# An FNet and gMLP block: another order of high parts, Gelus, copies and row sums in the z1 stage

## The chip, the cores and the metric

The kernel runs on one core of a Trainium2 chip. Its metric is the time of one execution on the device in microseconds (us); the median over several executions is given. The core has a matrix engine (PE in the profile, its weight loads PEld), a vector engine (DVE), a scalar engine for activations and copies (ACT), a general engine that here computes little and issues DMAs (POOL), and a sequencer that only issues DMAs (SP). Each engine works through its own queue in program order and waits on semaphores for what other engines must have done.

## The reference

Two sublayers act on 2048 tokens of 512 channels. What matters is the second one:

```python
h = _layernorm(x) * (1 + cb) + sb          # x after the Fourier sublayer
z  = _gelu(h @ w_in)                       # 2048 x 512 by 512 x 1792
z1 = z[..., :896]
z2 = _layernorm(z[..., 896:])
g  = w_sp @ z2 + b_sp[:, None]             # 2048 x 2048 by 2048 x 896
x  = x + gb * ((z1 * g) @ w_out)
```

The Fourier sublayer in front of it (two products with 512 x 512 matrices, two with 2048 x 2048 matrices) is the same in both kernels. All data are 32-bit floats.

## The kernel before, in words

**Split products.** Each float operand is split into a high part (a copy on ACT to a rounded type) and a low part (operand minus high part, a subtraction on DVE). `matmul3` (lines 93 to 97) then issues three PE instructions: high by high (L95), high by low (L96), low by high (L97). A high part and its low part must be there before the second or third of them can start.

**Stages.** The loop over `n` below `N2` is the Fourier sublayer. The loop from `N2` to `N3` computes z1 (lines 1156 to 1174), the next one z2, then come the product with `w_sp` and the output.

**The z1 stage.** The 896 columns of z1 are six column tiles of 128 and a seventh. The six are made as a 2 x 2 block product with seven block products in place of eight: the rows h (transposed, tiles `TT[k, g]`, k a block of 128 channels, g a group of 512 tokens) are cut into a, b, c, d by halves of channels and tokens, the weights into four blocks of 256 channels by 384 columns. The products run in the order `YPROD = (1, 2, 6, 7, 4, 5, 3)`, with four values of n each: step r below is n - N2 = r, and an even step multiplies one pair of h tiles (half gg = 0 or 1 of the token groups) with three column tiles, 18 PE instructions, in banks 0 to 2 of PSUM for gg = 0 and 3 to 5 for gg = 1. So steps 4 and 6 are product 2, steps 8 and 10 product 6, steps 12 and 14 product 7, steps 16 and 18 product 4, steps 20 and 22 product 5.

**The sums.** The weights' sums are `form_v`; their high and low parts `hi_v(p)` and `lo_v(p)`, two buffers in turn. The rows' sums are `make_x` (line 211; it also splits c for the seventh tile), `make_d`, S2 in `form_t` (line 245: d minus the difference a - c), `sum_x11` (a plus S2, needed by product 7) and a fourth sum, b minus S2, needed by product 4, which `prep_lo` makes at line 306 behind each low part of product 7. `prep_hi(m)` makes the high part of tile m, and with it a sum that it needs; `prep_lo(m)` the low part. `ahead(n)` calls `prep_hi` for steps n + 4 and n + 5.

**What comes out of PSUM.** After product 1 ACT copies the three banks away (L750) and they go on accumulating. After product 2 they hold z1 of the first token half: ACT applies Gelu and stores the result (L710, POOL issues the DMA), then copies product 1 back into the banks (L743), and product 6 is accumulated on top.

**The seventh column tile.** `mm_f7(g, k, ...)` accumulates it for token group g over four channel blocks, in bank `6 + g % 2`: groups 0 and 2 share bank 6, groups 1 and 3 bank 7. Groups 0 and 1 get their last blocks at the head of steps 4 and 6 and their Gelu is issued right there. `mm_x(gg)` does the first half of groups 2 and 3; it is called behind steps 6 and 10.

**The order** is written out by hand. `at(n, f, ...)` puts a call on a list (lines 1137 to 1155); a step runs its list, in the order in which it was filled, ahead of its matrix products, then `ahead`, then what empties PSUM, then the low parts of the next steps. A tile buffer or a PSUM bank that is given out again is waited for until its last readers are done.

Of the kernel before, what the change touches and what calls it, by code (L numbers as in the profile page):

```python
# [10 lines left out]
AF = mybir.ActivationFunctionType  # L11
ALU = mybir.AluOpType
# [7 lines left out]
def fnet_gmlp_kernel(  # L20
# [32 lines left out]
    nc = tc.nc  # L53
# [6 lines left out]
    ND = D // P  # L60
    NF = FH // P
# [17 lines left out]
    def bank(k, name):  # L79
        return psum.tile([P, 512], F32, tag=f"bank{k}", bufs=1, name=name)  # L80
# [12 lines left out]
    def matmul3(acc, ah, al, bh, bl, first, last, go_on=False):  # L93

        nc.tensor.matmul(acc, ah, bh, start=first, stop=False, skip_group_check=go_on)  # L95
        nc.tensor.matmul(acc, ah, bl, start=False, stop=False, skip_group_check=go_on)  # L96
        nc.tensor.matmul(acc, al, bh, start=False, stop=last, skip_group_check=go_on)  # L97
# [25 lines left out]
    def at(n, f, *a):  # L123
        fill.setdefault(n, []).append((f, a))

    def run(n):
        for f, a in fill.pop(n, []):
            f(*a)
# [10 lines left out]
    N2 = 4 * len(src)  # L139
    YPROD = (1, 2, 6, 7, 4, 5, 3)  # L140
    NY = {p: N2 + 4 * i for i, p in enumerate(YPROD)}
# [52 lines left out]
    def prep(n):  # L194

        if n not in prepared:
            prepared.add(n)
            prep_hi(n + 3)
            prep_lo(n + 2)

    def slot(i, name, dtype=F32):
        return slots[0].tile([P, Q], dtype, tag=f"slot{i}", bufs=1, name=name)

    slots, TT, S2, XH = [], {}, {}, {}
# [50 lines left out]
    def sum_x11(gg):  # L255
        for kk in range(2):
            nc.vector.tensor_tensor(TT[kk, gg], TT[kk, gg], S2[gg, kk], op=ALU.add)

    highs, lows, SE = set(), set(), []

    def load_first():
# [6 lines left out]
    def prep_hi(n):  # L268
        if n >= NE or n in highs:
            return  # L270
        highs.add(n)
        if N2 <= n < N4:
            T[n] = form_t(n)
        else:
            b, k = divmod(n, 4) if n < N2 else (NB0 + (n - N4) // 4, (n - N4) % 4)
            if b != NB0:
                T[n] = blocks.tile([P, Q], F32, tag="t", bufs=2, name=f"t{n}")
            if b == NB0:
                assert n in T
            elif n >= N4:  # L280
                squares(T[n], stage[b][:, k % 2], k // 2)
            else:
                squares(T[n], stage[b], k)
        AH[n] = SE[2][:, n - N4] if N4 <= n < N4 + 4 else blocks.tile([P, Q], F32R, tag="ah", bufs=4, name=f"ah{n}")
        nc.scalar.activation(AH[n], T[n], AF.Copy)  # L285
        if not N2 <= n < N4 and k == 3:
            stage.pop(b)
            if b != NB0:
                load(b + 2)


    def prep_lo(n):
        if n >= NE or n in lows:
            return
        lows.add(n)
        if N2 <= n < N4 and n % 4 == 3:
            AL[n] = slot(0, f"al{n}", F32R) if slots else zrow[0].tile([P, Q], F32R, tag="z1u", bufs=6, name=f"al{n}")
        elif N4 <= n < N4 + 4:
            AL[n] = slot(9 + n - N4, f"al{n}", F32R)
        else:  # L300
            AL[n] = blocks.tile([P, Q], F32R, tag="al", bufs=3, name=f"al{n}")
        t = T.pop(n)
        nc.vector.tensor_tensor(AL[n], t, AH[n].bitcast(F32), op=ALU.subtract)  # L303
        gg, kk = divmod(n % 4, 2)
        if NY[7] <= n < NY[7] + 4:
            nc.vector.tensor_tensor(TT[2 + kk, gg], TT[2 + kk, gg], S2[gg, kk], op=ALU.subtract)


    p2 = ctx.enter_context(ExitStack())
# [277 lines left out]
    def norm_y(t, i):  # L587
        LN[t, i] = rows.tile([P, D], F32, tag="row", bufs=6, name=f"h2_{t}_{i}")
        apply(LN[t, i], X.pop((t, i)), NRM.pop((t, i)))

    def post_h(t, i):
        h2 = LN.pop((t, i))
        nc.vector.tensor_tensor(h2, h2, mods[4], op=ALU.mult)
        (nc.vector if t == NQ - 1 else nc.gpsimd).tensor_tensor(h2, h2, mods[3], op=ALU.add)
        LN[t, i] = h2
# [12 lines left out]
    ZT = {}  # L608
# [73 lines left out]
    def ahead(n):  # L682
        for m in (n + 4, n + 5):
            prep_hi(m)

    ZB = (0, 1, 2, 6, 3, 4, 5, 7)
    Z1 = {}

    def mm_f7(g, k, th, tl):

        if k == 0:
            ZT["f7", g] = bank(6 + g % 2, f"f7p{g}")
        matmul3(ZT["f7", g], W7[0][:, 0, k], W7[0][:, 1, k], th, tl, k == 0, k == ND - 1)
        if k == ND - 1:
            end_z1(g, NF - 1, ZT.pop(("f7", g)), out_row(g, NF - 1))

    def out_row(g, f, tag="z1o"):
        if tag == "z1o":
            return zout[0].tile([P, Q], F32, tag=tag, bufs=7, name=f"z1o{g}_{f}")
        return zrow[0].tile([P, Q], F32, tag=tag, bufs=6, name=f"z1o{g}_{f}")  # L700

    def natural(z):
        return z.rearrange("p (a k i) -> p k a i", a=4, i=32)

    def turned(z):
        return z.rearrange("p (k a i) -> p k a i", k=4, i=32)

    def end_z1(g, f, ps, z):
        if ps is not None:
            nc.scalar.activation(natural(z), turned(ps), AF.Gelu_apprx_tanh)  # L710
        else:
            nc.scalar.activation(z, z, AF.Gelu_apprx_tanh)
        nc.gpsimd.dma_start(z1_d[g][f], z)

    def mm_x(gg):
        for kk, (h, l) in enumerate(XH.pop(gg)):
            mm_f7(2 + gg, kk, h, l)

    def mm_z1(n):
        p = YPROD[(n - N2) // 4]  # L720
        gg = n % 4 // 2
        fresh = p in (1, 5)
        a = [(AH.pop(m), AL.pop(m)) for m in (n, n + 1)]
        if p in (2, 3):
            for kk, t in enumerate(a):
                mm_f7(gg if p == 2 else 2 + gg, 2 + kk, *t)
        for f in range(3):
            if fresh:
                ZT[gg, f] = bank(3 * gg + f, f"z1p{p}_{gg}{f}")
            cols = slice(f * P, (f + 1) * P)  # L730
            for kk, (th, tl) in enumerate(a):
                matmul3(ZT[gg, f], WJ[1, p][:, 0, kk, cols], WJ[1, p][:, 1, kk, cols], th, tl,
                        fresh and kk == 0, kk == 1, not fresh)
        if n != N2 + 6:
            ahead(n)
        for f in range(3):
            empty_z1(p, gg, f)
        if p == 1:
            for kk, t in enumerate(a):
                mm_f7(gg, kk, *t)  # L740
        if p == 2:
            for f in range(3):
                nc.scalar.activation(turned(ZT[gg, f]), natural(Z1.pop((1, gg, f))), AF.Copy)  # L743

    def empty_z1(p, gg, f):

        ps = ZT[gg, f]
        if p in (1, 6, 7):
            Z1[p, gg, f] = zrow[0].tile([P, Q], F32, tag="z1u" if p == 6 else "z1m", bufs=6, name=f"z1_{p}_{gg}{f}")
            nc.scalar.activation(natural(Z1[p, gg, f]), turned(ps), AF.Copy)  # L750
        elif p in (2, 4):
            g, f = gg, f + (3 if p == 4 else 0)
            end_z1(g, f, ps, out_row(g, f, "z1u" if p == 2 else "z1o"))
        else:
            z = Z1.pop((7 if p == 5 else 6, gg, f))
            nc.vector.tensor_tensor(natural(z), turned(ps), natural(z), op=ALU.add)
            end_z1(2 + gg, f + (3 if p == 5 else 0), None, z)
# [287 lines left out]
    for j, turn, weigh, row, fold, hi in ((0, (25, 26, 27, 28), (29, 29, 30, 30), 26, (34, 34, 35, 36), (38, 35, 36, 37)),  # L1045
# [8 lines left out]
        n = weigh[3] + (3 if j == 0 else 1)  # L1054
# [13 lines left out]
    for t in range(NQ):  # L1068
        n = 8 * NQ * (t + 1)
# [43 lines left out]
    def change_s():  # L1113
        p2.close()
        slots.append(ctx.enter_context(pool("slots", "right")))
        spre.append(ctx.enter_context(pool("spre", "right")))
        bpool.append(ctx.enter_context(pool("bpool", "right")))
# [23 lines left out]
    at(N2 + 3, load_t, 3)  # L1141
    at(N2 + 4, make_x, 0)
    at(N2 + 6, make_d)
    at(N2 + 8, make_x, 1)
    at(N2 + 8, sum_x11, 0)
    at(N2 + 10, sum_x11, 1)
    at(N2 + 9, form_v, 5)
    at(N2 + 10, form_v, 3)
    for i, p in enumerate(YPROD[2:]):
        at(N2 + 4 + 4 * i, hi_v, p)  # L1150
        at(N2 + 5 + 4 * i, lo_v, p)
    at(N2 + 20, form_w, 7)
    at(NY[3], hi_w, 1)
    at(NY[3] + 1, lo_w, 1)
# [1 line left out]
    for n in range(N2, N3):  # L1156
        prep(n)
        if n % 2 == 0:
            prep_lo(n + 3)
        run(n)  # L1160
        if n % 2 == 0:
            mm_z1(n)
            ahead(n)
            if n == N2:
                norm_y(NQ - 1, 3)
            prep_lo(n + 4)
            prep_lo(n + 5)
            if n == N2:
                post_h(NQ - 1, 3)
                turn_h(NQ - 1, 3)  # L1170
                change_s()
                zout.append(w0.enter_context(pool("zout")))
            if n in (N2 + 6, N2 + 10):
                mm_x((n - N2) // 10)

    zstack = ctx.enter_context(ExitStack())
    w0.close()
# [14 lines left out]
    for i, p in enumerate(PROD):  # L1192
        for k in range(8):
            n = NB[p] + 2 * k
# [11 lines left out]
    for f in range(NF):  # L1206
        n = N4 + 24 + 8 * f
# [109 lines left out]
```

## Time and profile before

| | |
|---|---|
| time, median of 3 runs | 942.41 us (942.01 to 942.84) |
| the profiled execution's own time | 942.69 us |
| its span, first to last instruction | 940.9 us |
| PE busy | 932.1 us, 99% of the span |
| PEld busy | 772.7 us, 82% |
| DVE busy | 738.3 us, 78% |
| ACT busy | 413.6 us, 44% |
| POOL busy | 195.8 us, 21% |
| the z1 stage on PE | from 448.53 us to about 520 us |
| PE busy from 446 to 490 us | 41.55 of 44 us |
| PE busy from 490 to 528 us | 38.00 of 38 us |

A line of a timeline gives the start, the duration, the engine, the line of the kernel, the operation, the tiles (out<-in) and how many instructions were merged into it; brackets at its end give the idle time ahead of it and what ended it. Durations overlap: the distance from one start to the next is what an instruction costs its engine, unless it waits. A line of the waits gives who waited for whom, the total in us, how often, and the longest.

### The profile page before, as it was taken

How to read it: one execution, taken by the hardware profiler on the slowest of the kernel's cores; microseconds unless marked ns; L12 is line 12 of the kernel's file. 1: busy time of each engine (PE TensorE's matmuls, PEld its weight loads, DVE VectorE, ACT ScalarE, POOL GpSimd, SP SyncE). 2: the span in 40 equal slices, each digit the busy share in tenths (PEclk: the TensorE clock that was granted, in tenths of full speed). 3: DMA queues.
4: the chain of work that ended last, by engine and by line, in shares of the span. 5: the costliest groups of instructions: out<-in, count | busy, mean ns of one | idle time of the engine just before them, and what ended most of it. 6: DMA issues, size and time to landing. Idle time of an engine off the chain costs nothing.

```text
span 940.9 us, 12362 instructions
## 1 busy us (share of the span) xinstructions
PE 932.1 (99%) x4114; PEld 772.7 (82%) x4114; DVE 738.3 (78%) x1201; ACT 413.6 (44%) x726; POOL 195.8 (21%) x372
## 2 busy tenths in 40 slices
PE   9999999999999999999989999999999999999998
PEld 5888888888888888888868999888888888888886
DVE  6899957778677677875888878899799889886662
ACT  4684424232132222222577678675545544331221
POOL 2330000114554165323414211332000000000000
PEclk9999999999999999999999999999999999999999
DMA  9994762647539977994777523344564466743541
GB/s 213 226 235 103 143 146 67 168 134 180 144 87 321 275 212 216 275 332 151 240 264 278 180 95 74 90 100 104 133 142 106 114 145 139 182 110 140 185 173 56
DMA packets 236592, 157.07 MB, mean 167 GB/s; under 512 B 131472, under 2 KB 203408, under 8 KB 236400
## 3 DMA queue, kind: packets, MB, share of 16 engines
q1 hardware_dynamic: 223008, 118.65, 50.5%
q0 software_dynamic: 12128, 37.11, 11.0%
q8 instruction: 32, 0.52, 0.2%
q10 hardware_dynamic: 1392, 0.52, 0.2%
q14 instruction: 32, 0.26, 0.1%
HBM read 119.54 MB, written 36.70 MB: 166 GB/s over the span
## 4 chain that ended last, share of the span: by engine, by line
PE 92%; DVE 2%; DMA 2%; ACT 1%; POOL 1%; issue 1%; SPq 1%; DVEq 0%; ACTq 0%; POOLq 0%
PE gp L95 12%; PE gp L96 12%; PE gp L97 12%; PE gw L97 10%; PE gw L96 10%; PE gw L95 10%; PE op L96 3%; PE op L95 3%; PE op L97 3%; PE yp L97 3%; PE yp L96 3%; PE yp L95 3%; PE z2p L97 2%; PE z2p L95 2%; PE z2p L96 2%; PE z1p L97 1%
## 5 line engine op out<-in xcount | busy, mean ns | idle before, releaser
L285 ACT ACTIVATE ah<-t 128x512 fp32r<-128x512 f32 x244 | 154.1, 632 | 369.7 <-DVE t L190 240.6
L303 DVE TENSOR_TENSOR al<-t,ah 128x512 fp32r<-128x512 f32 x244 | 164.5, 676 | 65.3 <-PE gp L96 38.8
L95 PE MATMUL gp<-ah,hh 128*128 128x512 f32 x496 | 192.9, 389 | 0.0
L96 PE MATMUL gp<-al,hh 128*128 128x512 f32 x496 | 192.9, 389 | 0.0
L97 PE MATMUL gp<-ah,hl 128*128 128x512 f32 x496 | 192.9, 389 | 0.0
L190 DVE STREAM_TRANSPOSE t<-stage 128x512 f32<-128x512 f32 x236 | 165.9, 703 | 6.9 <-DMA stage<-in_A_dft_seq_re_dram 3.0
L96 PE MATMUL gw<-al,bh 128*128 128x512 f32 x400 | 155.6, 389 | 0.0
L97 PE MATMUL gw<-ah,bl 128*128 128x512 f32 x384 | 149.5, 389 | 0.0
L95 PE MATMUL gw<-ah,bh 128*128 128x512 f32 x384 | 149.4, 389 | 0.0
L97 PEld LDWEIGHTS gp<-ah,hl 128*128 128x128 f32 x496 | 93.1, 188 | 19.4
L95 PEld LDWEIGHTS gp<-ah,hh 128*128 128x128 f32 x496 | 93.1, 188 | 19.4
L96 PEld LDWEIGHTS gp<-al,hh 128*128 128x128 f32 x496 | 93.1, 188 | 19.2
L96 PEld LDWEIGHTS gw<-al,bh 128*128 128x128 f32 x400 | 75.1, 188 | 15.7
L97 PEld LDWEIGHTS gw<-ah,bl 128*128 128x128 f32 x384 | 72.1, 188 | 15.0 <-DVE bl L852 0.3
L95 PEld LDWEIGHTS gw<-ah,bh 128*128 128x128 f32 x384 | 72.1, 188 | 15.0
L824 POOL DMA_DIRECT2D s_d<-sj x64 | 35.1, 548 | 103.8 <-DVE sj L816 80.2
L95 PE MATMUL yp<-hth,gh 128*128 128x512 f32 x128 | 49.8, 389 | 0.0
L96 PE MATMUL yp<-htl,gh 128*128 128x512 f32 x128 | 49.8, 389 | 0.0
L97 PE MATMUL yp<-hth,gl 128*128 128x512 f32 x128 | 49.8, 389 | 0.0
L605 POOL DMA_DIRECT2D ht_d<-hturn x62 | 40.9, 665 | 23.6 <-DVE hturn L601 19.6
L95 PE MATMUL op<-woh,uh 128*128 128x512 f32 x112 | 43.6, 389 | 0.0
L96 PE MATMUL op<-wol,uh 128*128 128x512 f32 x112 | 43.6, 389 | 0.0
(220 smaller groups left out, 1466.4 us busy)
## 6 DMA issues: line engine op xcount, KB each, us to landing
stage<-in_A_dft_seq_im_dram SPq DMA_DIRECT2D x64, 256.0 KB, 5.2
sj<-in_B_w_sp_dram SPq DMA_DIRECT2D x32, 512.0 KB, 7.6
s_d<-sj POOLq DMA_DIRECT2D x64, 256.0 KB, 4.1
stage<-s_d SPq DMA_DIRECT2D x128, 128.0 KB, 2.7
stage<-in_A_dft_seq_re_dram SPq DMA_DIRECT2D x60, 256.0 KB, 5.3
stage<-in_B_w_sp_dram SPq DMA_DIRECT2D x88, 128.0 KB, 3.0
wm<-in_w_mod_dram SPq DMA_DIRECT2D x16, 256.0 KB, 5.8
xr<-in_A_x_dram POOLq DMA_DIRECT2D x16, 256.0 KB, 4.6
```

The lines of the kernel that those rows point to most:

```text
L95: nc.tensor.matmul(acc, ah, bh, start=first, stop=False, skip_group_check=go_on)
L96: nc.tensor.matmul(acc, ah, bl, start=False, stop=False, skip_group_check=go_on)
L97: nc.tensor.matmul(acc, al, bh, start=False, stop=last, skip_group_check=go_on)
L190: nc.vector.transpose(dst.rearrange("p (b i) -> p b i", i=32), block[:, :, 32 * k:32 * k + 32])
L285: nc.scalar.activation(AH[n], T[n], AF.Copy)
L303: nc.vector.tensor_tensor(AL[n], t, AH[n].bitcast(F32), op=ALU.subtract)
L605: eng.dma_start(v[a, i], ht[32 * a:32 * a + 32].rearrange("c (b r) -> c b r", r=32))
L824: nc.gpsimd.dma_start(s_d[m, r, g][b * P:(b + 1) * P, :], a)
```

## The change

Only the z1 stage changes, in five points.

- In `mm_z1` the high parts of the next pair (`ahead`) stand in front of the Gelus also at step 6, where they stood behind Gelus and copies.
- After product 2 each bank's copy stands right behind that bank's Gelu, in place of three Gelus and then three copies. The Gelu of the seventh tile for groups 0 and 1 is no longer issued where its products end, but behind the three Gelus and copies of its step (`end_f7`).
- The sum b minus S2 leaves `prep_lo` and becomes `sum_x12`, listed at steps 12 and 14.
- The weights' high and low part for product 6 move from steps 4 and 5 to step 3; the weight sums for products 5 and 3 from steps 9 and 10 to 13 and 17.
- The second `make_x` moves from step 8 to step 10, and the second `mm_x` from behind step 10 to behind step 12.

```diff
+    def sum_x12(gg):
+        for kk in range(2):
+            nc.vector.tensor_tensor(TT[2 + kk, gg], TT[2 + kk, gg], S2[gg, kk], op=ALU.subtract)
...
         nc.vector.tensor_tensor(AL[n], t, AH[n].bitcast(F32), op=ALU.subtract)
-        gg, kk = divmod(n % 4, 2)
-        if NY[7] <= n < NY[7] + 4:
-            nc.vector.tensor_tensor(TT[2 + kk, gg], TT[2 + kk, gg], S2[gg, kk], op=ALU.subtract)
...
         matmul3(ZT["f7", g], W7[0][:, 0, k], W7[0][:, 1, k], th, tl, k == 0, k == ND - 1)
-        if k == ND - 1:
-            end_z1(g, NF - 1, ZT.pop(("f7", g)), out_row(g, NF - 1))
+        if k == ND - 1 and g > 1:
+            end_f7(g)
+
+    def end_f7(g):
+        end_z1(g, NF - 1, ZT.pop(("f7", g)), out_row(g, NF - 1))
...
-        if n != N2 + 6:
-            ahead(n)
+        ahead(n)
         for f in range(3):
             empty_z1(p, gg, f)
+            if p == 2:
+                nc.scalar.activation(turned(ZT[gg, f]), natural(Z1.pop((1, gg, f))), AF.Copy)
         if p == 1:
             for kk, t in enumerate(a):
                 mm_f7(gg, kk, *t)
         if p == 2:
-            for f in range(3):
-                nc.scalar.activation(turned(ZT[gg, f]), natural(Z1.pop((1, gg, f))), AF.Copy)
+            end_f7(gg)
...
-    at(N2 + 8, make_x, 1)
     at(N2 + 8, sum_x11, 0)
     at(N2 + 10, sum_x11, 1)
-    at(N2 + 9, form_v, 5)
-    at(N2 + 10, form_v, 3)
+    at(N2 + 12, sum_x12, 0)
+    at(N2 + 14, sum_x12, 1)
+    at(N2 + 13, form_v, 5)
+    at(N2 + 17, form_v, 3)
     for i, p in enumerate(YPROD[2:]):
-        at(N2 + 4 + 4 * i, hi_v, p)
-        at(N2 + 5 + 4 * i, lo_v, p)
+        at(N2 + 4 + 4 * i - (not i), hi_v, p)
+        at(N2 + 5 + 4 * i - 2 * (not i), lo_v, p)
+    at(N2 + 10, make_x, 1)
...
-            if n in (N2 + 6, N2 + 10):
-                mm_x((n - N2) // 10)
+            if n in (N2 + 6, N2 + 12):
+                mm_x((n - N2) // 12)
```

## The prediction

> **What bounds the kernel now.** First the page: the share of PE, then the chain that ended last. Then the waits of PE's weight loads over the whole span, to see where PE is not busy.
>
> ```profile
> span 940.9 us, 12362 instructions
> PE 932.1 (99%) x4114; PEld 772.7 (82%) x4114; DVE 738.3 (78%) x1201; ACT 413.6 (44%) x726; POOL 195.8 (21%) x372
> ...
> PEld z1p L97 <- DVE vj L644: 1.8, 1, 1.8
> ...
> PEld z1p L95 <- ACT ah L285: 1.1, 1, 1.1
> PEld z1p L96 <- DVE al L303: 0.5, 1, 0.5
> PEld z1p L95 <- ACT z1p L743: 0.5, 1, 0.5
> ```
>
> PE is the bound: whatever PE loses anywhere adds to the end. Past its start it loses time in the z1 stage alone, at four places: a low weight part (`lo_v`), a high and a low row part behind S2, and a copy into PSUM. The change can win no more than these. What they cost is read from PE's timeline, start to start:
>
> ```profile
> 470.06 0.39 PE L97 MATMUL z1p<-ah,vj 128*128 128x512 f32 x1
> 470.29 0.39 PE L95 MATMUL f7p<-xh,w 128*128 128x512 f32 x1
> ...
> 471.42 0.39 PE L97 MATMUL f7p<-xh,w 128*128 128x512 f32 x1
> 471.89 0.50 PE L95 MATMUL z1p<-ah,vj 128*128 128x512 f32 x1
> 472.23 0.40 PE L96 MATMUL z1p<-al,vj 128*128 128x512 f32 x1
> ...
> 475.88 0.39 PE L97 MATMUL z1p<-ah,vj 128*128 128x512 f32 x1
> 476.98 0.50 PE L95 MATMUL z1p<-ah,vj 128*128 128x512 f32 x1 [0.72 <-ACT ah L285]
> 477.71 0.50 PE L96 MATMUL z1p<-al,vj 128*128 128x512 f32 x1 [0.23 <-DVE al L303]
> 478.05 0.39 PE L97 MATMUL z1p<-ah,vj 128*128 128x512 f32 x1
> ...
> 483.31 0.39 PE L96 MATMUL z1p<-al,vj 128*128 128x512 f32 x1
> 485.12 0.50 PE L97 MATMUL z1p<-ah,vj 128*128 128x512 f32 x1 [1.42 <-DVE vj L644]
> 485.45 0.39 PE L95 MATMUL z1p<-ah,vj 128*128 128x512 f32 x1
> ...
> 488.89 0.39 PE L95 MATMUL z1p<-ah,vj 128*128 128x512 f32 x1
> ```
>
> An undisturbed matmul takes 0.23 (470.06 to 470.29). The disturbed distances are 0.47, 0.34, 1.10, 0.73, 0.34, 1.81 and 0.33, together 5.12; less seven times 0.23 that is **3.51 us lost**. (The matmul behind each wait also takes 0.33 to 0.34: an extra 0.11 per stall.) That is the most the change can give back, 0.37%. At 488.89 step 14 begins; up to there both kernels give PE the same work, with the second `mm_x` at another place.
>
> **The change part by part.** The number of instructions on every engine stays the same; all is order. So I walk ACT's and DVE's queues in the new order, by these rows:
>
> ```profile
> 463.09 1.55 ACT L750 ACTIVATE z<-z1p 128x512 f32<-128x512 f32 x3
> 464.52 1.16 ACT L218 ACTIVATE xh<-tt 128x512 fp32r<-128x512 f32 x2
> 465.56 0.86 ACT L640 ACTIVATE vj<-w1e 128x768 fp32r<-128x768 f32 x1
> 466.30 0.61 ACT L710 ACTIVATE z1o<-f7p 128x512 f32<-128x512 f32 x1
> 468.66 1.24 ACT L285 ACTIVATE ah<-s 128x512 fp32r<-128x512 f32 x2 [1.75 <-DVE s L245]
> 469.80 1.56 ACT L710 ACTIVATE z1o<-z1p 128x512 f32<-128x512 f32 x3
> 471.23 1.65 ACT L743 ACTIVATE z1p<-z 128x512 f32<-128x512 f32 x3
> 472.79 0.60 ACT L710 ACTIVATE z1o<-f7p 128x512 f32<-128x512 f32 x1
> ```
>
> ```profile
> 465.19 0.69 DVE L221 TENSOR_TENSOR xl<-tt,xh 128x512 fp32r<-128x512 f32 x1 [1.18 <-ACT xh L218]
> ...
> 467.86 1.29 DVE L245 TENSOR_TENSOR s<-tt,tt 128x512 f32<-128x512 f32 x2
> ...
> 470.54 0.95 DVE L644 TENSOR_TENSOR vj<-w1e,vj 128x768 fp32r<-128x768 f32 x1
> 471.40 1.29 DVE L234 TENSOR_TENSOR xd<-xb,tt 128x512 f32<-128x512 f32 x2
> ```
>
> *Weights of product 6 at step 3.* `hi_v` now takes ACT at 464.52 in front of the two xh copies; it holds ACT for 0.74 (465.56 to 466.30) and ends 0.86 later, at 465.38. `lo_v` stands in front of xl on DVE, waits for that, starts at about 465.41 and holds DVE for 0.86 (470.54 to 471.40). So xl starts at 466.27 in place of 465.19: **1.08 later**, and with it the chain behind it, S2 (467.86 becomes 468.94), its high parts (468.66 becomes 469.74), and the first Gelu (469.80 becomes 470.88). The time won on DVE at 470.54 has no one waiting for it.
>
> *Gelu, copy, Gelu, copy.* A Gelu holds ACT for 0.48 (1.43 for three), a copy for 0.52 (1.56 for three), if they are independent. Now each copy overwrites the bank that the Gelu just ahead of it reads. What such a dependence costs on ACT is shown by the nearest pair, at the kernel's start, where the second line reads what the first wrote:
>
> ```profile
> 7.13 0.81 ACT L119 ACTIVATE xn<-x,first 128x511 f32<-128x511 f32 x1 [3.04 <-POOL xn L990]
> 7.97 0.63 ACT L459 ACTIVATE hh<-xn 128x512 fp32r<-128x512 f32 x1
> ```
>
> The second starts 0.03 behind the end of the first. A Gelu of 0.60 then holds ACT for 0.63; the lower bound is 0.48. I take 0.63: a pair 1.15, three pairs 3.45.
>
> *The seventh tile's Gelu goes behind them.* It was through at 466.9; now it starts at 470.88 + 3.45 = 474.33 and ends 0.61 later, at 474.94. Who waits for it is the point: the first `mm_x` (group 2) starts a new sum in bank 6, which this Gelu (group 0) still has to read. That `mm_x` ran at 470.29, and PE's queue holds steps 8 and 10 behind it. With 0.03 for the handoff it starts at 474.97. The distance on PE is 474.97 - 470.06 = 4.91, and the next 0.34; less two times 0.23, **4.79 us newly lost** (4.34 with the lower bound of 0.48).
>
> *What was late before.* Step 8's copies are now all done at about 474.4, before PE comes. Step 10's high parts stand ahead of its Gelus, at 474.33 + 0.48 = 474.81; its Gelus start 1.14 later (468.66 to 469.80), at 475.95, and its copies end by 479.5. PE gets to step 10 at 474.97 + 0.11 + 24 x 0.227 = 480.5. `lo_v` of product 7, freed of the weight sum and of the b sums in front of it, comes behind step 6's seventh Gelu (475.95 + 3.45 = 479.40): `hi_v` at 479.88, step 12's high parts 0.74 later, at 480.6, their low parts at 481.3, `lo_v` from 482.5 to 483.5; PE wants it at 480.5 + 18 x 0.227 + 0.45 = 485.0. So all the old 3.51 goes, under cover of the new wait.
>
> *The rest.* The b sums, four instructions of 0.69, and the second `make_x` go to steps at which only PE's own pace (18 matmuls, 4.1 us) frees buffers. The weight sum for product 3, 0.95 us long by the row below, now stands in front of product 5's `lo_v`:
>
> ```profile
> 483.24 0.95 DVE L631 TENSOR_TENSOR w<-w1e,w 128x768 f32<-128x768 f32 x1
> 484.11 0.95 DVE L644 TENSOR_TENSOR vj<-w,vj 128x768 fp32r<-128x768 f32 x1
> ...
> 498.53 0.95 DVE L644 TENSOR_TENSOR vj<-w,vj 128x768 fp32r<-128x768 f32 x1
> ```
>
> Before, this part was done at 499.48, and step 20 wanted it at 488.89 + 54 x 0.227 + 0.45 = 501.6: a margin of 2.1, of which 0.87 is spent. At zero, then, with 1.2 left over. The stores behind the Gelus on POOL's queue move by a few us, and nobody reads them before the output. SP's queue keeps its order.
>
> *The clock.* PE will stand idle from about 470.4 (end of the last matmul) to 474.97, some 4.5 us. The longest idle time after the start was the one ahead of 485.12, 1.42 by the row, and the matmuls behind it ran at full pace. What a long one does can be seen only at the program's start:
>
> ```profile
> L388 PEld LDWEIGHTS busyp<-busy,ones x10: 191/337/338, 1.5 to 8.1; 128*128 128x128 f32 x10
> ...
> 6.79 0.34 PEld L388 LDWEIGHTS busyp<-busy,ones 128*128 128x128 f32 x1 [0.52 <-issue]
> 7.64 0.23 PEld L388 LDWEIGHTS busyp<-busy,ones 128*128 128x128 f32 x1 [0.52 <-issue]
> ...
> L95 PEld LDWEIGHTS z1p<-ah,vj x84: 186/188/189, 448.3 to 519.3; 128*128 128x128 f32 x84
> ```
>
> A weight load took 337 ns, against 188 ns in the z1 stage, and the issue distance was 0.85 (6.79 to 7.64), then 0.46 (to 8.1): about half pace, from 1.5 to 7.6, although the granted clock reads 1.00 there. Half pace for 6.1 us costs 3.05 us. So for a restart after 4.5 us the bounds are 0 and 3.05. With an idle time three times the longest that did no harm I hold a slow restart the likelier, and a shorter one than after the load of the program: I take the middle, **1.5 us**.
>
> [...]
>
> **The sum.** - 3.51 + 4.79 + 1.5 = +2.8 us. The profiled execution took 942.69 us (span 940.9 and 1.8 around it), 0.3 above the median 942.41, so the steps carry over: 942.41 + 2.8 = **945.2 us**.
>
> **Rivals.** *B: the wait at bank 6 without a slow restart.* For it: no idle time in this trace after the start has been followed by slow matmuls. Against it: none was longer than 1.42. - 3.51 + 4.79 = +1.28, 943.7 us; 943.2 with the lower bound of 0.48.
>
> *C, not slower: the first `mm_x` finds its bank free.* Against it: the bank's number, 6 + g mod 2, is 6 for both groups. For it: the Gelu needs nothing but ACT's queue. Even then little is won: PE would run `mm_x` at 470.29, wait 0.6 for step 8's first copy (472.17), 0.9 for step 10's first copy (477.2), and 1.7 for `lo_v` of product 7 (483.5), since ACT and DVE are the slower chain here: 3.2 lost in place of 3.51, 942.1 us. It decides against a loss if the Gelu ends 1.3 earlier than walked, by 473.6; a gain above 0.2% would need `lo_v` earlier too.
>
> *D: product 5's `lo_v` becomes late.* DVE's queue from step 12 on now holds the b sums, both weight sums and the sums of `w_sp`. If a load makes one of those late by more than the 1.2 left, PE waits before step 20: each us beyond is a us, so 944.7 on top of B and 946.2 on top of my sum for one.
>
> **How the numbers follow.** My case 0.54, B 0.26, C 0.09, D 0.11. A measurement of this kernel tells about 0.2%, 1.9 us, from no change. My case and D are slower by more than that (0.65); B lies within it, as does nearly half of C (0.30); the rest of C is faster (0.05), if its chain is shorter than walked as well. The range goes from B's lower bound, 943.2 less 0.1, to my case with the whole 3.05, 946.7, and a little of D: 943.1 to 947.0; it leaves out C and part of D.
>
> **What would show it.** In the profile after: the first matmul of f7p with xh starts near 475.0, its wait put down to ACT and the tile z1o; the waits on vj, on ah and on al of product 6 are gone; weight loads behind 475 last 0.34 for some 3 us. S2 starts at 468.9. If the f7p matmul starts by 471, or a Gelu of f7p stands ahead of the copies on ACT, I am wrong in the main step; if weight loads behind it last 0.19, B holds; a wait of step 20 on vj is D.

## The result and the profile after

The changed kernel takes 945.81 us (median of 9 executions, 944.92 to 946.99), the kernel before 942.57 us (9 executions, 942.01 to 943.9): the ratio is 1.0032, with a 95% interval from 1.0023 to 1.0042. It is slower, by 3.2 us in the medians. Predicted were 945.2 us. The profiled execution took 945.12 us, 0.7 below the median.

The page of the changed kernel, its first lines, and the waits of PE's weight loads from 440 to 535 us, the z1 stage:

```profile
span 943.3 us, 12366 instructions
PE 932.5 (99%) x4114; PEld 774.0 (82%) x4114; DVE 738.2 (78%) x1201; ACT 414.4 (44%) x726; POOL 195.2 (21%) x372
```

```profile
PEld f7p L95 <- ACT z1o L714: 4.9, 1, 4.9
```

The four waits of before are gone. One has taken their place, and it is longer than they were together. Lines have moved by a few: the Gelus of L710 are L714 now, the copies of L743 are L742, the low parts of L303 are L307, the lines L285 are L289, L644 is L645. PE's timeline around that wait:

```profile
469.76 0.39 PE L97 MATMUL z1p<-ah,vj 128*128 128x512 f32 x1
474.60 0.50 PE L95 MATMUL f7p<-xh,w 128*128 128x512 f32 x1 [4.45 <-ACT z1o L714]
474.93 0.47 PE L96 MATMUL f7p<-xl,w 128*128 128x512 f32 x1
475.19 0.63 PE L97 MATMUL f7p<-xh,w 128*128 128x512 f32 x1
475.62 0.63 PE L95 MATMUL f7p<-xh,w 128*128 128x512 f32 x1
...
478.18 0.56 PE L95 MATMUL z1p<-ah,vj 128*128 128x512 f32 x1
478.58 0.40 PE L96 MATMUL z1p<-al,vj 128*128 128x512 f32 x1
478.81 0.40 PE L97 MATMUL z1p<-ah,vj 128*128 128x512 f32 x1
```

The first `mm_x` (f7p with xh) stands 4.84 us behind the last matmul of step 6, and the next one 0.33 behind it: 4.84 + 0.33 less two times 0.23 is 4.71 us lost. Then come eight distances of 0.40 to 0.43 (475.19 to 478.58 is 3.39 us in place of 1.84): another 1.55 us. The clock shows it as well, in the table by stretches (the stretch, its length, PE's busy time and matmuls, weight loads, DVE, ACT, POOL, the granted clock, the DMA share and rate):

```profile
470.00:474.60 4.60, 0.15 (x2) 0.01 (x1) 3.70 (x6) 4.50 (x10) 1.68 (x3) 1.00 0.93 251
...
475.20:478.60 3.40, 3.40 (x10) 2.66 (x9) 2.40 (x4) 3.31 (x7) 1.26 (x3) 0.51 1.05 414
478.60:482.00 3.40, 3.40 (x16) 2.79 (x15) 0.02 (x1) 2.29 (x5) 1.08 (x2) 1.00 1.04 411
```

For 3.4 us PE had half the clock (0.51 from 475.20 to 478.60). In the page's 40 slices, where the clock stays at 9 tenths or more throughout, this cannot be seen. What PE waited for is on ACT, here in the new order:

```profile
464.16 0.85 ACT L641 ACTIVATE vj<-w1e 128x768 fp32r<-128x768 f32 x1
464.89 1.16 ACT L218 ACTIVATE xh<-tt 128x512 fp32r<-128x512 f32 x2
469.38 1.23 ACT L289 ACTIVATE ah<-s 128x512 fp32r<-128x512 f32 x2 [3.33 <-DVE s L245]
470.52 0.58 ACT L714 ACTIVATE z1o<-z1p 128x512 f32<-128x512 f32 x1
471.13 0.60 ACT L742 ACTIVATE z1p<-z 128x512 f32<-128x512 f32 x1
471.67 0.58 ACT L714 ACTIVATE z1o<-z1p 128x512 f32<-128x512 f32 x1
...
473.96 0.58 ACT L714 ACTIVATE z1o<-f7p 128x512 f32<-128x512 f32 x1
474.44 1.14 ACT L289 ACTIVATE ah<-s 128x512 fp32r<-128x512 f32 x2
```

and, ahead of its high parts of S2, on DVE:

```profile
465.05 0.96 DVE L645 TENSOR_TENSOR vj<-w1e,vj 128x768 fp32r<-128x768 f32 x1 [1.35 <-ACT vj L641]
465.92 0.69 DVE L221 TENSOR_TENSOR xl<-tt,xh 128x512 fp32r<-128x512 f32 x1
...
468.58 1.29 DVE L245 TENSOR_TENSOR s<-tt,tt 128x512 f32<-128x512 f32 x2
```

The seventh tile's Gelu (z1o from f7p) runs from 473.96 to 474.54, and 0.06 later PE goes on. From 469.38 on ACT works with no gap over 0.03: that Gelu waits for nothing but its turn.

### The profile page after: what moved, and what is told of

It reads as the page before. It is cut to its first block, busy times and chain, and to the rows that moved or that the text cites. A ratio compares the mean times of both kernels' runs of the same rounds, so it can differ in the third digit from the quotient of the medians.

```text
span 943.3 us, 12366 instructions
## 1 busy us (share of the span) xinstructions
PE 932.5 (99%) x4114; PEld 774.0 (82%) x4114; DVE 738.2 (78%) x1201; ACT 414.4 (44%) x726; POOL 195.2 (21%) x372
## 4 chain that ended last, share of the span: by engine, by line
PE 93%; DVE 3%; ACT 1%; issue 1%; POOL 1%; DMA 1%; SPq 0%; ACTq 0%; DVEq 0%; POOLq 0%
PE gp L97 12%; PE gp L95 12%; PE gp L96 12%; PE gw L97 10%; PE gw L96 10%; PE gw L95 10%; PE op L97 3%; PE op L95 3%; PE op L96 3%; PE yp L97 3%; PE yp L95 3%; PE yp L96 2%; PE z2p L97 2%; PE z2p L96 2%; PE z2p L95 2%; PE z1p L95 1%
## 5 line engine op out<-in xcount | busy, mean ns | idle before, releaser
L289 ACT ACTIVATE ah<-t 128x512 fp32r<-128x512 f32 x244 | 154.0, 632 | 370.9 <-DVE t L190 240.3
L307 DVE TENSOR_TENSOR al<-t,ah 128x512 fp32r<-128x512 f32 x244 | 164.3, 675 | 63.4 <-PE gp L96 37.3
```

## The experiments

All medians are given with the ratio to the kernel before, which ran beside them on the same chip.

**The seventh tile's Gelu back at its old place.** The change otherwise as it is.

```diff
-        if k == ND - 1 and g > 1:
+        if k == ND - 1:
             end_f7(g)
...
         if p == 2:
-            end_f7(gg)
```

> The changed kernel, with the seventh tile's Gelu of groups 0 and 1 again where its products end, ahead of the Gelus and copies of its step. My theory (the first mm_x waits for that Gelu at bank 6, and the long wait brings the slow restart): mm_x runs without a wait, no weight load in the z1 stage lasts over 0.2 us, and three short waits are left: 0.5 for step 8's first copy, 0.9 for step 10's first copy, 1.2 for the low weights of product 7, 2.7 us lost in place of 3.5 in the kernel before: 0.8 us below the kernel before, some 941.7. Rival 1 (the loss comes from the weights of product 6 in front of the xh copies, 1.1 us on the whole chain): still at least 1 us above the kernel before, 943.6 or more. Rival 2 (copies that alternate with Gelus cost ACT too much): above the kernel before as well.

Measured: 941.9 us, ratio 0.9992 (0.9983 to 1.0001), against 942.58. The waits of the weight loads in the z1 stage:

```profile
PEld z1p L95 <- ACT z1p L742: 1.9, 2, 1.0
PEld z1p L97 <- DVE vj L645: 0.9, 1, 0.9
PEld z1p L95 <- ACT z L752: 0.6, 1, 0.6
```

The long wait is gone with this one instruction's place, and no weight load of the stage lasts over 189 ns. These waits are longer than what PE loses, as in the changed kernel, where the weight load waited 4.9 us and PE stood idle for 4.45. Start to start, as in the prediction, PE lost 0.7 at step 8, 0.9 at step 10, 0.5 at step 12, whose banks had to be copied out, and 0.8 for product 7's low weights. That is 2.8 us where 2.7 were reckoned, though the parts were reckoned as 0.5, 0.9, none and 1.2; the time is within 0.2 us of the one expected. Rivals 1 and 2, which keep the loss, fall.

**The first `mm_x` behind step 10.** The same wait seen from PE's side: ACT and DVE keep the changed order.

```diff
-            if n in (N2 + 6, N2 + 12):
+            if n in (N2 + 10, N2 + 12):
```

> The changed kernel, with the first mm_x behind step 10 in place of step 6; ACT and DVE keep the changed order. My theory: PE no longer holds steps 8 and 10 behind bank 6; step 8 waits 1.9 us for its first copy, step 10 0.9 for its, product 7's low weights 0.3: 3.1 us lost in place of 3.5, 0.4 us below the kernel before, some 942.2, and no slow weight loads, since no wait is longer than 2 us. Rival 1 (the order on ACT is what costs): as the changed kernel, 943.7 or more. Rival 2 (the slow restart has another cause than the length of the wait): slow weight loads of 0.33 us here too, 943.8.

Measured: 942.15 us, ratio 0.9997 (0.9989 to 1.0006). The profiled execution, at 943.36 the slowest of eleven, had one wait in the stage, and slow matmuls behind it:

```profile
PEld z1p L95 <- ACT z1p L742: 2.3, 1, 2.3
```

```profile
473.00:476.40 3.40, 3.40 (x9) 2.65 (x8) 2.06 (x4) 3.37 (x7) 1.62 (x3) 0.50 0.92 293
476.40:480.00 3.60, 3.60 (x17) 2.93 (x16) 1.64 (x3) 3.50 (x8) 1.62 (x3) 1.00 1.05 418
```

So the loss of the change sits in what PE holds in line behind bank 6, not in ACT's order. My expectation that no slow loads come behind a wait of some 2 us held in ten of eleven executions, by their mean clock, and failed in the profiled one.

**The sums alone,** in the kernel before.

```diff
-        gg, kk = divmod(n % 4, 2)
-        if NY[7] <= n < NY[7] + 4:
-            nc.vector.tensor_tensor(TT[2 + kk, gg], TT[2 + kk, gg], S2[gg, kk], op=ALU.subtract)
...
-    at(N2 + 9, form_v, 5)
-    at(N2 + 10, form_v, 3)
+    at(N2 + 12, sum_x12, 0)
+    at(N2 + 14, sum_x12, 1)
+    at(N2 + 13, form_v, 5)
+    at(N2 + 17, form_v, 3)
```

> The kernel before with one part of the change alone: the sum b minus S2 as a function of its own at steps 12 and 14, and the weight sums of products 5 and 3 at steps 13 and 17. My theory: the low weights of product 7 come 2.1 us earlier on DVE, the 1.8 us wait of step 12 goes, the other three waits stay: 1.7 us below the kernel before, some 940.9, ratio 0.998. Rival (the wait only moves, to the low weights of product 5 at step 20 or to step 16's high parts): within 0.5 us of the kernel before, with a new wait of PE between 489 and 503.

Measured: 941.03 us, ratio 0.9984 (0.9975 to 0.9993).

```profile
PEld z1p L95 <- ACT ah L289: 1.1, 1, 1.1
PEld z1p L96 <- DVE al L307: 0.5, 1, 0.5
PEld z1p L95 <- ACT z1p L744: 0.4, 1, 0.4
...
PEld z1p L97 <- DVE vj L645: 0.2, 1, 0.2
```

The wait on product 7's low weights falls from 1.8 to 0.2, the other three stay, and no new one comes later. This part of the change is worth 1.5 us by itself.

**Idle times of several lengths,** in the kernel before: at eight values of n the high part is copied again, up to 26 times, to the same values. The extra copies make the time of this kernel meaningless.

```diff
-        nc.scalar.activation(AH[n], T[n], AF.Copy)
+        for _ in range(1 + {80: 16, 92: 20, 108: 24, 120: 18, 214: 22, 230: 26, 246: 17, 262: 21}.get(n, 0)):
+            nc.scalar.activation(AH[n], T[n], AF.Copy)
```

> The kernel before, with eight places (four in the Fourier stage, four in the product with w_sp) at which one high part is copied 16 to 26 times more by ACT, to the same values, so that PE runs out of high parts and stands idle for some 1 to 8 us, a different length at each place. Nothing else is changed, so what follows the idle time is PE's own. [...] Rival (the slow loads in the changed kernel come from something else, as a collision at bank 6): weight loads of 0.19 behind every idle time.

Measured: the repeated copies took longer than reckoned, so the nine long idle times came out between 3.5 and 12.3 us, and the short end was not covered. Pairs of stretches, each an idle time and what followed it (the columns are length, PE busy and matmuls, granted clock, DMA share and rate):

```profile
387.20:391.20 4.00, 0.57 (x3) 1.00 0.00 0
391.20:396.00 4.80, 4.50 (x12) 0.69 0.12 48
751.40:763.70 12.30, 0.50 (x3) 0.64 0.22 50
763.70:768.30 4.60, 4.54 (x10) 0.50 0.00 0
808.20:812.90 4.70, 0.56 (x3) 0.99 0.01 3
812.90:816.00 3.10, 3.08 (x6) 0.50 0.02 5
520.40:522.40 2.00, 0.57 (x4) 1.00 1.04 405
522.40:527.00 4.60, 4.60 (x20) 1.00 0.53 206
```

Slow matmuls came behind every idle time of 3.5 us or more, none behind the 1.9 us of the z1 stage (the last pair). They came in two quite different stages. At seven of the nine places PE waited for a high part and no bank, so a collision at bank 6 is not their cause, and the rival falls; at two, ending at 280.92 and 412.19, it waited for a subtraction that empties a bank of another stage (gl<-gp, L91). Behind 12.3 us the clock had fallen during the idle time (0.64 in the mean of 751.40 to 763.70); behind 3.9 us it fell only 1.8 us after PE had gone on (weight loads of 0.19 us from 391.28, of 0.33 from 393.09).

**The weights of product 6 back at steps 4 and 5.**

```diff
-        at(N2 + 4 + 4 * i - (not i), hi_v, p)
-        at(N2 + 5 + 4 * i - 2 * (not i), lo_v, p)
+        at(N2 + 4 + 4 * i, hi_v, p)
+        at(N2 + 5 + 4 * i, lo_v, p)
```

> The changed kernel, with the high and low weights of product 6 again at steps 4 and 5. [...] Rival (the weights' place is free, since ACT and DVE had idle time there): as the changed kernel, 945.8.

Measured: 944.43 us, ratio 1.0021 (1.0011 to 1.003). The wait at bank 6 is 1.1 us shorter than in the changed kernel, 3.8 in place of 4.9:

```profile
PEld f7p L95 <- ACT z1o L714: 3.8, 1, 3.8
```

Ten executions fall in three groups by their mean clock: one at 1.0 with 942.73, five at 0.998 with 943.91 to 944.44, four at 0.996 with 945.25 to 945.53. The first is near the sum without a slow restart, an estimate: the 942.51 of the kernel before beside it, less 3.51, and 3.62 lost at bank 6 in the profiled execution (470.13 to 473.87 and the next 0.34, less two times 0.23), give 942.62. The steps between the groups are some 1.5 and 1.2 us. By the 1.55 us that a slow stretch of 3.4 us cost in the changed kernel, one such stretch and two would fit, again an estimate; the profiled execution, at 944.42, has one, with eight weight loads of 0.33 us from 475.19 on.

**The seventh tile's Gelu behind the first Gelu and copy.**

```diff
                 nc.scalar.activation(turned(ZT[gg, f]), natural(Z1.pop((1, gg, f))), AF.Copy)
+                if f == 0:
+                    end_f7(gg)
...
-        if p == 2:
-            end_f7(gg)
```

> The changed kernel, with the seventh tile's Gelu behind the first pair of Gelu and copy in place of the third. Instructions on all engines are the same, two pairs of ACT work change places with one Gelu. My theory (what counts is when bank 6 comes free, and a long wait costs more than its length): mm_x starts 2.3 us earlier, PE is idle for some 2.2 us, mostly without a slow restart, and product 7's low weights are waited for by 0.8: 3.3 us lost in place of 3.5, some 942.4, which is 3.4 us below the changed kernel although only 2.3 us of wait are gone. Rival (the slow restart has nothing to do with the length of the wait): 2.3 less 0.8, so some 1.5 us below the changed kernel, 944.3, with slow weight loads behind the wait.

Measured: 942.87 us, ratio 1.0002 (0.9993 to 1.0011), 2.9 us below the changed kernel.

```profile
PEld f7p L95 <- ACT z1o L714: 2.6, 1, 2.6
PEld z1p L97 <- DVE vj L645: 0.9, 1, 0.9
```

The waits are those of the walk. The half microsecond above 942.4 is the clock: four executions at 0.999 or 1.0 took 942.07 to 942.77, seven at 0.998 took 942.87 to 943.15. So "mostly without a slow restart" was wrong: seven of eleven have the mean clock of one slow stretch. That they took only some 0.7 us more than the others would fit a slow stretch that costs the 1.55 us of the changed kernel and covers the 0.9 of the wait for product 7's low weights, an estimate; no trace of one of them shows it. In the profiled execution, at 942.39, no weight load behind the wait is slow (0.19 us each), so the rival fails there.

**One part alone: step 10's high parts in front,** in the kernel before.

```diff
-        if n != N2 + 6:
-            ahead(n)
+        ahead(n)
```

> The kernel before with one part of the change alone: at step 6 the high parts of step 10 stand in front of the Gelus and copies. My theory (ACT and DVE are the slower chain up to step 12): the waits of step 10 on its high and low parts go (1.5 us), its first copy is waited for instead (0.5), and the 0.9 us won is given back at step 12, since the low weights of product 7 come no earlier on DVE: that wait grows from 1.8 to some 2.7 us, and the time is that of the kernel before, 942.5, within 0.3. Rival (waits of PE add up, each one removed is won): 0.9 us below the kernel before, 941.6, with step 12's wait still at 1.8.

Measured: 944.22 us, ratio 1.0015 (1.0006 to 1.0024): neither.

```profile
PEld z1p L97 <- DVE vj L644: 2.7, 1, 2.7
PEld z1p L95 <- ACT z1p L742: 1.3, 2, 0.8
```

The waits are as walked: those on step 10's high and low parts are gone, the copy is waited for, and product 7's low weights by 2.7 in place of 1.8. The time is not: two of eleven executions took 942.29 and 942.95 at a clock of 1.0, the other nine 943.87 to 945.38 at 0.998 to 0.996. Nothing was won on PE's way, and with the longer wait came the slow clock: in the profiled execution the weight loads last 0.33 from 486.76 on, for one stretch of 3.4 us. In the medians 1.7 us were lost.

**A version from the findings:** the changed kernel with the seventh tile's Gelu at its old place, the weights of product 6 at steps 4 and 5, and the low weights of product 7 at step 8, in front of step 12's low parts on DVE.

```diff
-        if k == ND - 1 and g > 1:
+        if k == ND - 1:
             end_f7(g)
...
         if p == 2:
-            end_f7(gg)
...
-        at(N2 + 4 + 4 * i - (not i), hi_v, p)
-        at(N2 + 5 + 4 * i - 2 * (not i), lo_v, p)
+        at(N2 + 4 + 4 * i, hi_v, p)
+        at(N2 + 5 + 4 * i - (p == 7), lo_v, p)
```

> The changed kernel with three places changed: the seventh tile's Gelu for groups 0 and 1 where its products end, the high and low weights of product 6 at steps 4 and 5, and the low weights of product 7 at step 8 right behind their high part, in front of step 12's low parts on DVE. My theory (bank 6 and the 1.1 us of the weights are what the change loses, its other parts win): mm_x and step 8 run without a wait, step 10 waits 0.7 for its first copy, step 12 0.5 for the copies out of its banks: 1.2 us lost in place of 3.5, some 940.3, ratio 0.9975. Rival (the alternation of Gelus and copies or the later sums cost as much as they win): 941.5 or more.

Measured: 939.74 us, ratio 0.9971 (0.996 to 0.9983): faster than both kernels, 2.8 us below the one before.

```profile
PEld z1p L95 <- ACT z L752: 0.6, 1, 0.6
PEld z1p L95 <- ACT z1p L742: 0.5, 1, 0.5
```

Two short waits are left, 0.5 at step 10 and 0.6 at step 12, where 0.7 and 0.5 were expected. The rest of the change, the alternation of Gelus and copies included, is in this version, so the rival falls; what the alternation is worth by itself was not run.

## Why the prediction was right

**The old waits.** All 3.51 us of them went, as walked: none is in the waits after.

**The chain on ACT and DVE.** Steps here start earlier than in the profile before: 0.30 us on PE (step 6's last matmul at 469.76 in place of 470.06), 0.36 on ACT (the second pair's high parts at 461.67 in place of 462.03). With 0.36 taken off, the walk's xl at 466.27, S2 at 468.94, its high parts at 469.74, the first Gelu at 470.88, the seventh tile's Gelu at 474.33 and the `mm_x` at 474.97 are 465.91, 468.58, 469.38, 470.52, 473.97 and 474.61. Measured: 465.92, 468.58, 469.38, 470.52, 473.96 and 474.60. A Gelu whose bank the next copy overwrites held ACT for 0.61 (470.52 to 471.13; 0.63 taken, the lower bound was 0.48), and a pair took 1.15.

**The wait at bank 6.** 4.79 us predicted, 4.71 measured. Moving either side of it, the Gelu or the `mm_x`, took the loss away, 3.9 and 3.7 us in the medians.

**The slow restart.** 1.5 us was taken as the middle between 0 and 3.05, and no row spoke for the middle. That it was 1.55 in the profiled execution is luck; what holds of the argument is that a slow restart was the likelier case. In the median it is more: 3.24 less the 1.20 of the waits (4.71 - 3.51) is 2.0 us. Four of nine executions had a mean clock of 0.998 and took 944.92 to 945.2, five had 0.996 and took 945.81 to 946.99. This term was undersized by some 0.5 us, which is most of the distance from 945.2 to 945.81. Rival B, with no slow restart, is out: none of the nine had a clock above 0.998. (The granted clock of 1.00 that the prediction read at the program's start is no measurement: that trace's clock records begin at 7.72 us, and the 1.00 that the profile reads from 3.00 to 7.50 stands where it has none.)

**Product 7's low weights** came at 483.27, 0.7 to 1.1 later than walked: step 12's high parts waited 1.06 for PE, which was itself late by the slow clock. It cost nothing, as PE was later still.

**Rivals C and D.** C's bank is not free, and its point that little would be won without that wait is what the first experiment shows (0.7 us below the kernel before, 0.3 reckoned). D's wait at step 20 is not there: the sums have room at their new places.

## What to carry to other kernels

Before an instruction that frees a PSUM bank or a buffer is moved back in a queue, look up who is given that bank next and where it stands in its own queue: here one Gelu of 0.6 us, for which no one had waited before, held up 36 matmuls that had nothing to do with it. Parts of a reordering do not add up where two engines form the slower chain: sums alone won 1.5 us, while high parts in front alone only moved PE's waits and, with one longer wait, lost 1.7. And several short waits of PE were cheaper here than one long one of the same sum: the four of the kernel before, 3.9 us together, went with 942.5 us, the one of 3.8 with the weights of product 6 back with 944.4. So look at how long each wait is, not only at their total.

## What the runs showed of the hardware

In these runs the slow clock was rare up to a longest wait of 2.3 us (1 of 11 executions there) and frequent from 2.6 us on (7 of 11). By the longest wait of the weight loads in the z1 stage, and the executions whose mean granted clock was 0.998 or less:

| kernel | longest wait, us | executions at 0.998 or less |
|---|---|---|
| version from the findings | 0.6 | 0 of 6 |
| Gelu back at its old place | 1.0 | 1 of 11 |
| sums alone | 1.1 | 1 of 11 |
| before, beside the experiments | 1.8 | 1 of 63 |
| first `mm_x` behind step 10 | 2.3 | 1 of 11 |
| Gelu behind the first pair | 2.6 | 7 of 11 |
| high parts in front, alone | 2.7 | 9 of 11 |
| weights of product 6 back | 3.8 | 9 of 10 |
| changed kernel | 4.9 | 9 of 9 |

Why two kernels with waits of some 1 us have one such execution each is not shown.

Four of the profiled executions without added idle time have one slow stretch in the z1 stage, of eight weight loads of 0.30 to 0.33 us. It begins at 475.20 in the changed kernel (wait 4.9), at 475.19 with the weights of product 6 back (3.8), at 486.76 with the high parts in front alone (2.7) and at 473.04 with the first `mm_x` behind step 10 (2.3). The clock records of the changed kernel's trace give full clock for 467.63 us, half for 3.41 and full for 464.21.

The longest wait alone does not tell what one execution does. The lines below are stretches of the first `mm_x` behind step 10 (two) and of the Gelu behind the first pair (two), each a stretch in which PE mostly waited and one behind it; the columns are those of the table of the changed kernel:

```profile
469.80:472.20 2.40, 0.59 (x3) 0.17 (x1) 2.22 (x4) 2.34 (x5) 0.36 (x1) 1.00 0.88 264
473.00:476.40 3.40, 3.40 (x9) 2.65 (x8) 2.06 (x4) 3.37 (x7) 1.62 (x3) 0.50 0.92 293
470.00:472.70 2.70, 0.63 (x3) 0.19 (x1) 2.52 (x5) 2.67 (x6) 0.59 (x1) 1.00 0.90 298
473.50:477.00 3.50, 3.50 (x17) 2.85 (x16) 2.15 (x5) 3.44 (x7) 1.30 (x4) 1.00 1.02 379
```

Behind the wait of 2.3 us the clock was 0.50, behind the longer one of 2.6 it was 1.00. What decides between the two is not shown.

In the changed kernel the slow stretch lasted 3.4 us and cost some 1.5 us; the execution had a mean clock of 0.998. Half clock for 3.41 of 943.3 us lowers the mean by 0.002, so mean clocks of 0.996 would fit two such stretches, an estimate; no trace of such an execution was kept.
